# W' from high and low halves in three float32r passes instead of one float32 pass, its depth sum split in two

## The chip, the cores and the metric

The program runs on one core of a Trainium2 chip. The metric is device time in microseconds (us): the median of three runs. The profile is of one further execution; its span is the time from its first instruction to its last.

## The reference, cut to what matters

A clustered attention is followed by two feed-forward blocks. The change is in the last: `moe2_w3` and `moe2_w_out` are multiplied with nothing between them, so that the kernel may form their product first.

```python
def _moe2_ref(x, w1, w2, w3, w_out):      # x: 1536 x 512
    a = x @ w1                            # 512 x 1024
    b = x @ w2                            # 512 x 1024
    h = a * b @ w3                        # 1024 x 1024
    return (h @ w_out).astype(np.float32) # 1024 x 512
```

Ahead of it stand, for each of 2 batches, 8 heads of 768 rows and 64 columns: scores of q and k, masked to equal clusters, an exponential, a product with v; and a first feed-forward block `g(x @ w_in) @ w_out` with `g(h) = h` above 1, `(h + 1)^2 / 4` between, 0 below -1. The weights of both blocks come as 64-bit floats.

## The kernel before, in words

**Stages.** Attention of batch 0 is computed first (4 units of two heads, 48 score tiles of 128 x 768). Then the matmuls of both feed-forward blocks for batch 0 (line L1254) run between the score tiles of batch 1, and then those for batch 1 (L1254 and, in a form with fewer products, L1507). L1254 of batch 0 needs the whole of batch 0's attention.

**A score tile** is: four matmuls into PSUM (L853, TensorE, "PE"), a row maximum (L861, VectorE, "DVE"), a bias (L866, GpSimd, "POOL"), the exponential (L874, ScalarE, "ACT"), six transposes (L891, PE), a copy of the result to `pt` (ACT or DVE). Six tiles make a group, after which L962 multiplies with v (24 matmuls into `av`).

**Weights.** A chunk of 128 x 512 weights is loaded as 64-bit words (`w64`) and turned into float32 in `wf` by five instructions: absolute value of the high word (ACT, L1107), clamp (L1111), rebase (L1117) and sign (L1123) on DVE, low word by DVE (L1129) or by ACT and POOL (L1136, L1140). Where a chunk is used in float32r (a float32 that TensorE reads at less than full precision), it is split: the high half is a copy to float32r (`hi`, L347 on ACT or L349 on DVE), the low half is the chunk less its high half (`lo`, L352 on POOL or DVE), both in a `whl` tile. Three matmuls, high-high, high-low and low-high (`PASSES`), then stand for one float32 product (`mm4`, L1254).

**W'.** The product `w3 @ w_out` (1024 x 512) is made during batch 0's attention, in 8 blocks `m` of 128 rows, each in two steps `hf` of four depth tiles (`wp_mm`, L1198). The steps are in full float32: the chunk of w3 in `wf`, `w_out` in the tile `wo2` (8 depth tiles, 128 x 512 float32). The two steps of a block add up in one PSUM bank (`mo`), a copy takes it to `wf` (`wp_copy`), a DMA to the DRAM tensor `wp` (`wp_put`, L1211); the output matmuls read it back much later. PE's time for one step is that of 4 matmuls (the trace has 2 records for each, so x8).

**What sets the order.** Every operation is entered in a plan with its needs; the order in which all are issued, and for operations with two possible engines the engine, stand in a table written out in the program (`ORDER`). Each engine runs its part in that order and waits at each instruction for what it needs. DMAs are issued from ACT's queue (weights) and SP's (the rest).

## Time and profile before

| | |
|---|---|
| median of 3 runs | 726.48 us (725.79 to 728.29) |
| profiled execution | 725.32 us |
| its span | 723.6 us |
| PE, weight loads, DVE busy | 704.4, 617.9, 615.9 us |
| ACT, POOL busy | 465.5, 285.3 us |

Busy time is the union of an engine's instructions. Two records of one engine can overlap: the next starts before the last result is out. PEld is PE's loading of weights, which runs beside its matmuls. The chain of waits goes back from the last instruction to whatever let each step start; of it 89% is PE.

### The profile page before, as it was taken

Reading aid. Unit: us, or ns where it says so; the run is one execution under the profiler, and the core shown is the slowest. Engines: PE = TensorE matmul, PEld = TensorE weight load, DVE = VectorE, ACT = ScalarE, POOL = GpSimd, SP = SyncE. Lnnn points to the kernel's source line nnn. Section 1 sums busy time; section 2 is a strip of 40 time slices with the busy share of each in tenths; the row PEclk is TensorE's granted clock in tenths of the full one; section 3 lists DMA queues with packets and bytes.
Section 4 is the critical chain, followed back from the end, with each engine's and each line's share of the span. In section 5 each row is a group of like instructions: output and inputs, shape, how many; then the busy total and the mean of one; then the engine's idle time right before and its main releaser. Section 6 shows DMA issues by size and latency. Waiting matters only on the chain.

```text
span 723.6 us, 11965 instructions
## 1 busy us (share of the span) xinstructions
PE 704.4 (97%) x4144; PEld 617.9 (85%) x4145; DVE 615.9 (85%) x1134; ACT 465.5 (64%) x870; POOL 285.3 (39%) x358
## 2 busy tenths in 40 slices
...
GB/s 312 135 193 131 194 192 272 202 191 201 205 166 199 171 175 217 233 235 187 244 217 225 205 230 157 186 164 152 46 103 57 59 88 59 44 72 74 73 52 80
DMA packets 113932, 115.80 MB, mean 160 GB/s; under 512 B 74128, under 2 KB 82768, under 8 KB 113872
## 3 DMA queue, kind: packets, MB, share of 16 engines
...
q8 instruction: 32, 0.52, 0.3%
...
## 4 chain that ended last, share of the span: by engine, by line
PE 89%; DVE 4%; ACT 3%; DMA 2%; issue 1%; SPq 0%; POOL 0%; ACTq 0%; POOLq 0%; DVEq 0%
PE mo L1254 36%; PE sc L1507 9%; PE sc L853 9%; PE mo L1198 7%; PE mo L1507 5%; PE sc L891 5%; PE sc L1254 5%; PE av L962 4%; PE av L970 3%; PE av L1507 2%; PE av L1254 2%; DMA vn<-phl 1%; DMA kq<-in_qT_dram 1%; DVE nm L861 1%; ACT pt L347 1%
## 5 line engine op out<-in xcount | busy, mean ns | idle before, releaser
L1254 PE MATMUL mo<-X,whl 128*128 128x384 f32 x924 | 169.5, 338 | 0.0
L1254 PEld LDWEIGHTS mo<-X,whl 128*128 128x128 f32 x924 | 159.5, 188 | 2.3 <-issue 0.6
L1254 PE MATMUL mo<-G,whl 128*128 128x384 f32 x732 | 133.2, 337 | 0.0
L1254 PEld LDWEIGHTS mo<-G,whl 128*128 128x128 f32 x732 | 126.6, 188 | 0.9 <-DVE X L352 0.3
L861 DVE TENSOR_REDUCE nm<-sc 128x1 f32<-128x768 f32 x96 | 90.2, 952 | 15.9 <-PE sc L853 13.6
L352 POOL TENSOR_TENSOR whl<-wf,whl 128x512 fp32r<-128x512 f32 x48 | 63.3, 1319 | 73.1 <-ACT whl L347 44.6
L1140 POOL TENSOR_TENSOR wf<-wf,w 128x512 int32<-128x512 int32 x32 | 42.2, 1320 | 80.4 <-DVE wf L1123 32.1
L866 POOL TENSOR_SCALAR nm<-nm 128x1 f32<-128x1 f32 x96 | 26.3, 274 | 102.9 <-DVE nm L861 94.2
L347 ACT ACTIVATE whl<-wf 128x512 fp32r<-128x512 f32 x76 | 47.5, 627 | 29.4 <-PE mo L1254 11.8
L853 PE MATMUL sc<-k,q 128*128 128x512 f32 (+1 forms) x192 | 55.1, 368 | 3.8 <-DVE nm L861 1.6
L1198 PE MATMUL mo<-wo,wf 128*128 128x512 f32 x128 | 58.0, 596 | 0.0
L874 ACT ACTIVATE P<-sc,nm 128x768 f32<-128x768 f32 x56 | 50.1, 898 | 10.6 <-POOL nm L866 5.5
L347 ACT ACTIVATE pt<-sc 128x768 f32<-128x768 f32 (+1 forms) x50 | 39.4, 807 | 18.6 <-PE sc L891 14.7
L853 PE MATMUL sc<-kq 80*128 80x512 f32 (+1 forms) x192 | 49.7, 340 | 0.0
L891 PEld LDWEIGHTS sc<-ident,P 128*128 128x128 f32 x336 | 37.9, 141 | 12.5 <-issue 4.9
L1107 ACT ACTIVATE wf<-w 128x512 f32<-128x512 f32 x64 | 42.4, 672 | 5.7 <-POOL wf L1140 1.7
L891 PE MATMUL sc<-ident,P 128*128 128x128 f32 x336 | 43.9, 275 | 1.6 <-DVE nm L861 1.3
L1123 DVE SCALAR_TENSOR_TENSOR wf<-w,wf 128x512 uint32<-128x512 uint32 x64 | 44.2, 693 | 0.9
L874 ACT ACTIVATE sc<-sc,nm 128x768 f32<-128x768 f32 x40 | 34.7, 868 | 15.5 <-POOL nm L866 15.4
L1198 PEld LDWEIGHTS mo<-wo,wf 128*128 128x128 f32 x128 | 23.3, 190 | 24.5 <-issue 23.7
L352 DVE TENSOR_TENSOR phl<-sc,phl 128x768 f16<-128x768 f32 x40 | 38.1, 952 | 5.6 <-ACT phl L347 5.2
L853 PEld LDWEIGHTS sc<-k,q 128*128 128x128 f32 x192 | 31.4, 189 | 12.2 <-DVE nm L861 3.0
...
## 6 DMA issues: line engine op xcount, KB each, us to landing
wf<-wd ACTq DMA_DIRECT2D x64, 256.0 KB, 2.7
...
wd<-wf SPq DMA_DIRECT2D x48, 256.0 KB, 3.6
...
wf<-wp ACTq DMA_DIRECT2D x16, 256.0 KB, 2.9
...
```

The source lines that it names most:

```text
L347: nc.scalar.activation(out=out, in_=in_, func=AF.Copy)
L352: (nc.gpsimd if e == "POOL" else nc.vector).tensor_tensor(out=out, in0=a, in1=b, op=ALU.subtract)
L853: nc.tensor.matmul(ps[:, n], q[0:n_rows, q0:q0 + 128], k[0:n_rows, n], start=first, stop=not first)
L861: nc.vector.tensor_reduce(out=nm, in_=T[("sc", b), s], axis=AX.X, op=ALU.max, negate=True)
L874: nc.scalar.activation(out=new(("P", b), s).rearrange("p n s -> p (n s)") if by_pe(s) else T[("sc", b), s], in_=T[("sc", b), s], func=AF.E ...
L891: nc.tensor.transpose(T[("sc", b), s][:, c], p[:, c], ident)
L1107: nc.scalar.activation(out=T["wf", i], in_=T[w64, i].bitcast(F32)[:, :, 1], func=AF.Abs)
L1123: nc.vector.scalar_tensor_tensor(out=w, in0=T[w64, i][:, :, 1], scalar=0xC0000000, in1=w, op0=ALU.bitwise_and, op1=ALU.bitwise_or)
L1140: nc.gpsimd.tensor_tensor(out=w, in0=w, in1=T[w64, i].bitcast(I32)[:, :, 0], op=ALU.add)
L1198: nc.tensor.matmul(acc, w[:, k4 * 128:(k4 + 1) * 128], wo2[:, hf * 4 + k4], start=(hf == 0 and k4 == 0), stop=(hf == 1 and k4 == 3),)
L1254: nc.tensor.matmul(acc, w[:, a, k4 * 128:(k4 + 1) * 128], rhs(c, k4), start=(first and k4 == 0 and n == 0), stop=(last and k4 == 3 and n = ...
L1507: nc.tensor.matmul(ps, lhs(av, a, k), rhs(bv, c, k), start=k == 0 and n == 0, stop=k == 1 and n == 2,)
```

## The change

The steps of W' run in three float32r passes. The chunks of w3 (16) and of w_out2 (8) are split into halves: 24 more copies and 24 more subtractions. Split w_out2 takes twice the room, so that the depth sum is made in two parts: first `hf` 0 of all 8 blocks, then `hf` 1. The first part is copied from PSUM to `wf` and stored in a DRAM tensor `wp0`; it is loaded back, added to the second part on DVE, and stored in `wp`. Only four split depth tiles are kept at a time: two in parts of `X0` that attention fills later (its last two units now wait for the first part), the others in tiles of their own. `ORDER` is another table.

In the order, `sc` tiles are scores, `mo` the PSUM bank of W', `X_75` and `wo_119` to `wo_122` the homes of split w_out2; lines of the changed kernel are 6 higher for the operations of attention. On PE, a place behind the third product with v, before:

```order
L891 MATMUL sc_178<-ident,P_108 128x128 x6
L1198 MATMUL mo_123<-wo_118,wf 128x512 x4
L891 MATMUL sc_177<-ident,P_106 128x128 x6
L891 MATMUL sc_177<-ident,P_107 128x128 x6
L1198 MATMUL mo_123<-wo_118,wf 128x512 x4
L783 MATMUL sc_178<-ident,raw_91 128x128 x6
L853 MATMUL sc_177<-k_98,q_101 128x512
```

and in the changed kernel:

```order
L897 MATMUL sc_181<-ident,P_107 128x128 x6
L897 MATMUL sc_182<-ident,P_109 128x128 x6
L1194 MATMUL mo_127<-X_75,whl 128x512 x6
L1194 MATMUL mo_127<-wo_119,whl 128x512 x3
L1194 MATMUL mo_127<-wo_120,whl 128x512 x3
L897 MATMUL sc_181<-ident,P_108 128x128 x6
L859 MATMUL sc_182<-k_99,q_102 128x256
```

A step is 4 float32 matmuls before and 12 float32r matmuls now, with as many transposes around it.

On DVE, in the fifth group of score tiles (between the 25th and the 26th row maximum, L861 and L867), before:

```order
L861 TENSOR_REDUCE nm<-sc_178 128x1
L1111 TENSOR_SCALAR wf<-wf 128x512
L1117 TENSOR_SCALAR wf<-wf 128x512
L1123 SCALAR_TENSOR_TENSOR wf<-w_115,wf 128x512
L1129 SCALAR_TENSOR_TENSOR wf<-w_115,wf 128x512
L1111 TENSOR_SCALAR wf<-wf 128x512
L352 TENSOR_TENSOR X_75<-av,X_75 128x384
L1111 TENSOR_SCALAR wf<-wf 128x512
L1117 TENSOR_SCALAR wf<-wf 128x512
L1123 SCALAR_TENSOR_TENSOR wf<-w_111,wf 128x512
L861 TENSOR_REDUCE nm<-sc_177 128x1
```

and now:

```order
L867 TENSOR_REDUCE nm<-sc_182 128x1
L355 COPY rb<-mo_127 128x384
L1132 SCALAR_TENSOR_TENSOR wf<-w_112,wf 128x512
L987 TENSOR_TENSOR av<-av,rb 128x384
L358 TENSOR_TENSOR k_100<-kq_118,k_100 64x768
L358 TENSOR_TENSOR whl<-wf,whl 128x512
L358 TENSOR_TENSOR wo_122<-wf,wo_122 128x512
L358 TENSOR_TENSOR q_103<-kq_118,kq_106 64x768
L936 TENSOR_SCALAR su<-su 128x6
L937 RECIPROCAL rc<-su 128x6
L1114 TENSOR_SCALAR wf<-wf 128x512
```

Low halves (L358 to `whl` and `wo`) stand between the conversions, the row maxima and the work on k and q.

On ACT, in the same group, before:

```order
L347 ACTIVATE wf<-mo_123 128x512
L874 ACTIVATE P_106,su<-sc_177,nm 128x768
L347 ACTIVATE vn<-sc_178 128x768
L347 ACTIVATE rb<-mo_123 128x384
L347 ACTIVATE pt_96<-sc_177 128x768
L1136 ACTIVATE w_115<-w_115 128x512
L874 ACTIVATE P_107,su<-sc_177,nm 128x768
L874 ACTIVATE P_108,su<-sc_178,nm 128x768
```

and now:

```order
L353 ACTIVATE whl<-wf 128x512
L353 ACTIVATE pt_97<-sc_182 128x768
L880 ACTIVATE P_107,su<-sc_182,nm 128x768
L353 ACTIVATE kq_106<-kq_118 64x768
L353 ACTIVATE wf<-mo_127 128x512
L1139 ACTIVATE w_112<-w_112 128x512
L353 ACTIVATE rb<-mo_127 128x384
L1104 DMA w_115<-in_w_out_dram 128x1024
L353 ACTIVATE whl<-wf 128x512
```

High halves (L353 `whl<-wf`) and further copies of k and q stand between the exponentials (L880) and the copies to `pt`.

Between the 6th and the 30th tile the order has on DVE 8 more low halves, 1 more high half, 3 more copies from PSUM to `wf` and 8 more conversion instructions; on ACT 12 more high halves, 6 more copies of k and q and 3 more absolute values. Between the 30th and the 48th tile it has on DVE the 8 additions, and 2 copies to `wf`, 3 copies to `pt` and 2 low parts of k and q fewer; on ACT 7 more high halves and 3 more copies to `pt`. On PE the 16 steps stand 8 and 8 in both stretches, before and now. Of the 24 low halves 11 are on DVE and 13 on POOL; of the 24 high halves 21 on ACT and 3 on DVE.

```diff
--- before.py
+++ after.py
@@ -36,63 +36,65 @@
...
 ORDER = (
-    "##$V$.$0$4#%#*$X$2#,#0$]#.$Z%s%X%V%Z#(%e#2#4%h%k$6%c$_%y&,%r:m%_$H$8%m$::|$a;.$<%a;<$q%|$c$>%i#_$J&%#i#e$e%u"
...
+    "###%#<#*$X$V$.$0#,#0$4$2#.%X:m%V%e#(#2%[#4%c%q%h$6$8%_;%$:%y%m%b$_%|&#$H$<$Z$]$q%i%]$a$c#:#c$>:o;6$@$e$B$F&,"
...
@@ -192,6 +194,7 @@
     tri = const.tile([128, 128], BF16, name="tri")
     half = const.tile([128, 1], F32, name="half")
     nbig = const.tile([128, 1], F32, name="nbig")
+    wp0 = dram.tile([KF2, 128, DM], F32, name="wp0")
     wp = dram.tile([DM // 128, 128, KF2, 128], F32, name="wp")
     xd = dram.tile([KD, 128, S], F32, name="xd")
 
@@ -217,7 +220,10 @@
             RINGS[r, b] = len(BUFS[r, b])
     mask0 = early_p.tile([128, 2, 2, TG], F32R, name="mask0")
     kq0 = early_p.tile([128, 2, NP, S], F32, name="kq0")
-    wo2 = early_p.tile([128, KF2, DM], F32, name="wo2")
+    BUFS["wo2"] = [early_p.tile([128, 2, DM], F32R, name=f"wo2{i}") for i in range(KF2 // 2)]
+    RINGS["wo2"] = KF2 // 2
+    BUFS["wo2x"] = [X0[:, :, j, :DM] for j in (KD - 1, KD - 2)]
+    RINGS["wo2x"] = 2
     late = {}
 
 
@@ -284,7 +290,7 @@
     ROWS, ROW, MASK = ((0.45, 1.24),), ((0.45, 0.57),), ((0.75, 0.45),)
     MOVES = {
         "c_load": ((0.45, 0.18),), "al": ROWS, "ul": ROWS, "vl": ROWS, "ap": ROWS, "vT": ((0.62, 2.7),),
-        "sT": ((0.62, 2.7),), "k2": ROW * 2 + MASK, "wps": ((0.45, 1.05),), "wd": ((0.45, 1.05),),
+        "sT": ((0.62, 2.7),), "k2": ROW * 2 + MASK, "wps": ((0.45, 1.05),), "wps0": ((0.45, 1.05),), "wpl": ((0.45, 1.05),), "wd": ((0.45, 1.05),),
         "xs": ROW, "xr": ROW, "os": ROW,
     }
 
@@ -1070,7 +1076,7 @@
             nm = ("x", u, g)
             add(("xm", u, g), {"DVE": 0.5}, p + 3.0, x_mul(u, g), [("pv", u, g), ("ri", u, g)], [("tmp", nm)] if b else [], [("av", (u, g)), ("rb", (u, g))] if b else [("rb", (u, g))], near=("av", (u, g)))
             if b == 0:
-                add_split("x", nm, p + 3.5, lambda a, j=j, g=g: X0[:, a, j, cols(g)], [("xm", u, g)], "av", (u, g))
+                add_split("x", nm, p + 3.5, lambda a, j=j, g=g: X0[:, a, j, cols(g)], [("xm", u, g)] + ([("wp", m, 0) for m in range(KF2)] if j >= KD - 2 else []), "av", (u, g))
             else:
                 add(("xs", u, g), {"DMA": 0.5}, p + 4.0, to_dram(nm, xd[j, :, cols(g)]), [("xm", u, g)], frees=[("tmp", nm)])
 
@@ -1082,13 +1088,13 @@
 
 
     nchunk = [0]
-    N_EARLY = 2 * KF2 + wo2.shape[1] + AHEAD
+    N_EARLY = 3 * KF2 + AHEAD
     c64 = []
 
     def low_by_pool(i):
         return i % 2 == 0
 
-    def chunk(t, src, is64, split=True, dst=None, needs=(), keep=None):
+    def chunk(t, src, is64, split=True, halves="whl", needs=(), keep=None):
         i = nchunk[0]
         nchunk[0] += 1
         w64 = ("w64", 0 if i < N_EARLY else 1)
@@ -1100,10 +1106,7 @@
                 nc.scalar.dma_start(out=new("wf", i), in_=src)
 
         def absv(e):
-            if dst is None:
-                new("wf", i)
-            else:
-                T["wf", i] = dst
+            new("wf", i)
             nc.scalar.activation(out=T["wf", i], in_=T[w64, i].bitcast(F32)[:, :, 1], func=AF.Abs)
 
         def clamp(e):
@@ -1143,10 +1146,10 @@
             nc.sync.dma_start(out=wd[keep], in_=T["wf", i])
 
         def hi(e):
-            copy(e, new("whl", i)[:, 0], T["wf", i])
+            copy(e, new(halves, i)[:, 0], T["wf", i])
 
         def lo(e):
-            w = T["whl", i]
+            w = T[halves, i]
             sub(e, w[:, 1], T["wf", i], f(w)[:, 0])
 
         if is64:
@@ -1158,7 +1161,7 @@
             if before is not None:
                 needs = list(needs) + [(LAG_W, ("wc", before, 3))]
             add(("wl", i), {"ACT": 0.2}, t - 14.0, load, list(needs) + W_AFTER[i:i + 1], [(w64, i)], behind="w64", moves=((0.46, 1.8),))
-            add(("wabs", i), {"ACT": 0.56}, t - 9.0, absv, [("wl", i)], [] if dst is not None else [("wf", i)], behind="wf")
+            add(("wabs", i), {"ACT": 0.56}, t - 9.0, absv, [("wl", i)], [("wf", i)], behind="wf")
             add(("wc", i, 0), {"DVE": 0.34, "POOL": (1.92, LATE)}, t - 8.6, clamp, [("wabs", i)])
             add(("wc", i, 1), {"DVE": 0.34}, t - 8.2, rebase, [("wc", i, 0)])
             add(("wc", i, 2), {"DVE": 0.6}, t - 7.8, top, [("wc", i, 1)])
@@ -1174,36 +1177,45 @@
             add(("wl", i), {"ACT": 0.2}, t - 12.0, load, needs, [("wf", i)], behind="wf", moves=((0.46, 1.05),))
             last = ("wl", i)
         if split:
-            add(("whi", i), {"ACT": 0.52, "DVE": (0.34, LATE)}, t - 5.0, hi, [last], [("whl", i)], behind="whl")
+            add(("whi", i), {"ACT": 0.52, "DVE": (0.34, LATE)}, t - 5.0, hi, [last], [(halves, i)], behind=halves)
             add(("wlo", i), {"POOL": 1.3, "DVE": (0.61, LATE)}, t - 4.0, lo, [("whi", i)], frees=[("wf", i)])
         return i
 
 
 
-    W_ACC = [("mo", 0), "av", ("sc", 0), ("sc", 0)][:W_SIDE] + [("mo", 0)] * (KF2 - W_SIDE)
-
-    def wp_acc(m, first=False):
-        ring, name = W_ACC[m], ("wp", m)
-        t = new(ring, name) if first else T[ring, name]
-        if ring == ("sc", 0):
-            o = 0 if where[ring, name] % PER[0] == 0 else S - 512
-            t = t[:, o:o + 512]
-        return t
-
-    def wp_mm(i, m, hf):
-        def fn(e):
-            w = T["wf", i]
-            acc = wp_acc(m, hf == 0)
+    def wo2_home(kt):
+        return "wo2x" if kt < 2 else "wo2"
+
+    def wp_mm(i, m, hf, x):
+        def fn(e):
+            w, acc = T["whl", i], new(("mo", 0), ("wp", m, hf))
             for k4 in range(4):
-                nc.tensor.matmul(
-                    acc, w[:, k4 * 128:(k4 + 1) * 128], wo2[:, hf * 4 + k4],
-                    start=(hf == 0 and k4 == 0), stop=(hf == 1 and k4 == 3),
-                )
-        return fn
-
-    def wp_copy(m):
-        def fn(e):
-            copy(e, new("wf", ("wp", m)), wp_acc(m))
+                for n, (a, c) in enumerate(PASSES):
+                    nc.tensor.matmul(
+                        acc, w[:, a, k4 * 128:(k4 + 1) * 128], T[wo2_home(hf * 4 + k4), x[k4]][:, c],
+                        start=(k4 == 0 and n == 0), stop=(k4 == 3 and n == 2),
+                    )
+        return fn
+
+    def wp_part(m):
+        def fn(e):
+            copy(e, new("wf", ("wp0", m)), T[("mo", 0), ("wp", m, 0)])
+        return fn
+
+    def wp_keep(m):
+        def fn(e):
+            nc.sync.dma_start(out=wp0[m], in_=T["wf", ("wp0", m)])
+        return fn
+
+    def wp_back(m):
+        def fn(e):
+            nc.sync.dma_start(out=new("wf", ("wp", m)), in_=wp0[m])
+        return fn
+
+    def wp_add(m):
+        def fn(e):
+            w = T["wf", ("wp", m)]
+            nc.vector.tensor_tensor(out=w, in0=w, in1=T[("mo", 0), ("wp", m, 1)], op=ALU.add)
         return fn
 
     def wp_put(m):
@@ -1215,30 +1227,28 @@
 
     dt = DT_W
     wo2_chunks = []
-    steps = [(m, hf) for hf in range(2) for m in range(W_SIDE)] + [(m, hf) for m in range(W_SIDE, KF2) for hf in range(2)]
+    WO2_AT = {0: range(4), 3: (4,), 5: (5,), 8: (6, 7)}
+    steps = [(m, hf) for hf in range(2) for m in range(KF2)]
     for n, (m, hf) in enumerate(steps):
         t = T_W + dt * n
-        if m == 0:
-            for kt in range(hf * 4, hf * 4 + 4):
-                wo2_chunks.append(chunk(t - 10.0 + 2.0 * (kt % 4), w_out2[kt], True, False, wo2[:, kt]))
-        i = chunk(t, w3T[m, hf], True, False)
-        needs = [("wc", i, 3)] + [("wc", x, 3) for x in wo2_chunks[hf * 4:hf * 4 + 4]]
-        if hf:
-            needs.append(("wp", m, 0))
-        elif W_ACC[m] == ("sc", 0):
-            needs.append(("am", 0, "q", NP - 1))
+        for kt in WO2_AT.get(n, ()):
+            wo2_chunks.append(chunk(t - 10.0 + 2.0 * (kt % 4), w_out2[kt], True, True, wo2_home(kt)))
+        x = wo2_chunks[hf * 4:hf * 4 + 4]
+        i = chunk(t, w3T[m, hf], True, True)
+        acc = (("mo", 0), ("wp", m, hf))
         add(
-            ("wp", m, hf), {"PE": 3.44}, t, wp_mm(i, m, hf), needs,
-            [(W_ACC[m], ("wp", m))] if hf == 0 else [], [("wf", i)],
+            ("wp", m, hf), {"PE": 2.8}, t, wp_mm(i, m, hf, x), [("wlo", i)] + [("wlo", y) for y in x],
+            [acc], [("whl", i)] + [(wo2_home(hf * 4 + k4), y) for k4, y in enumerate(x)],
         )
         while ahead and len(ahead) * 2 * KF2 > AHEAD * (2 * KF2 - 1 - n):
             x, src = ahead.pop(0)
             chunk(t + dt / 2, src, True, False, keep=x)
-        if hf:
-            add(
-                ("wpe", m), {"ACT": 0.5, "DVE": (0.61, LATE)}, t + dt, wp_copy(m), [("wp", m, 1)],
-                [("wf", ("wp", m))], [(W_ACC[m], ("wp", m))],
-            )
+        if hf == 0:
+            add(("wpe0", m), {"ACT": 0.5, "DVE": (0.61, LATE)}, t + dt, wp_part(m), [("wp", m, 0)], [("wf", ("wp0", m))], [acc])
+            add(("wps0", m), {"DMA": 0.5}, t + dt + 2.0, wp_keep(m), [("wpe0", m)], frees=[("wf", ("wp0", m))])
+        else:
+            add(("wpl", m), {"DMA": 0.5}, t - 4.0, wp_back(m), [("wps0", m)], [("wf", ("wp", m))])
+            add(("wpe", m), {"DVE": 0.61}, t + dt, wp_add(m), [("wp", m, 1), ("wpl", m)], frees=[acc])
             add(("wps", m), {"DMA": 0.5}, t + dt + 2.0, wp_put(m), [("wpe", m)], frees=[("wf", ("wp", m))])
 
 
```

## Rows read from the trace of the kernel before

**Rows 1.** Five stretches of the program: busy time by engine (clock, DMA share, GB/s last)
```profile
core 0: us, PE busy (x) PEld busy (x) DVE busy (x) ACT busy (x) POOL busy (x), PEclk, DMA share, GB/s
0.00:44.00 44.00, 30.94 (x207) 21.99 (x209) 35.01 (x76) 36.01 (x55) 16.46 (x28) 1.00 0.61 209
44.00:127.00 83.00, 82.75 (x427) 52.38 (x424) 73.58 (x121) 70.23 (x121) 27.86 (x41) 1.00 0.61 202
127.00:200.00 73.00, 72.01 (x387) 42.50 (x388) 65.81 (x111) 53.61 (x94) 18.16 (x30) 1.00 0.64 199
200.00:475.00 275.00, 273.53 (x1729) 257.25 (x1728) 244.27 (x416) 198.94 (x367) 117.85 (x141) 1.00 0.86 200
475.00:723.60 248.60, 245.16 (x1403) 243.78 (x1402) 197.21 (x413) 106.71 (x236) 104.96 (x120) 1.00 0.26 82
```

**Rows 2.** Chain of waits, 93 to 202 us: start us, length us, what
```profile
93.11 3.66 PE mo L1198 x8
96.77 1.31 PE sc L891 x12
98.08 3.44 PE mo L1198 x8
...
115.75 0.69 PE sc L853 x4
...
122.94 0.81 ACT pt L347
123.78 0.85 ACT kq L347
...
187.92 3.44 PE mo L1198 x8
...
200.07 2.11 PE mo L1254 x12
```

**Rows 3.** Groups by line: operation, tiles, shapes, count | busy us, mean ns | idle before
```profile
L1254 PE MATMUL mo<-X,whl 128*128 128x384 f32 x924 | 169.5, 338 | 0.0
L1254 PEld LDWEIGHTS mo<-X,whl 128*128 128x128 f32 x924 | 159.5, 188 | 2.3 <-issue 0.6 <-DVE tmp L1279 0.3 <-ACT tmp L347 0.3
L352 POOL TENSOR_TENSOR whl<-wf,whl 128x512 fp32r<-128x512 f32 x48 | 63.3, 1319 | 73.1 <-ACT whl L347 44.6 <-DVE whl L349 18.8 <-issue 5.6
L347 ACT ACTIVATE whl<-wf 128x512 fp32r<-128x512 f32 x76 | 47.5, 627 | 29.4 <-PE mo L1254 11.8 <-PE sc L1254 4.8 <-PE mo L1507 4.0
L352 DVE TENSOR_TENSOR whl<-wf,whl 128x512 fp32r<-128x512 f32 x48 | 34.5, 721 | 1.9 <-ACT whl L347 1.8
L1107 ACT ACTIVATE wf<-w 128x512 f32<-128x512 f32 x64 | 42.4, 672 | 5.7 <-POOL wf L1140 1.7 <-issue 1.0 <-DVE whl L352 0.8
L1123 DVE SCALAR_TENSOR_TENSOR wf<-w,wf 128x512 uint32<-128x512 uint32 x64 | 44.2, 693 | 0.9
L1111 DVE TENSOR_SCALAR wf<-wf 128x512 f32<-128x512 f32 x61 | 26.1, 429 | 2.8 <-ACT wf L1107 2.0 <-POOL G L352 0.4 <-issue 0.2
L1289 DVE TENSOR_TENSOR Yp<-Yp,mo 128x384 f32<-128x384 f32 x29 | 15.4, 545 | 0.0
L347 ACT ACTIVATE kq<-kq 64x768 fp32r<-64x768 f32 x17 | 14.2, 840 | 0.6 <-PE sc L853 0.3
```

**Rows 4.** Waits of VectorE, then of ScalarE, 44 to 127 us: total us, times, longest
```profile
DVE nm L861 <- PE sc L853: 5.3, 6, 1.2
ACT pt L347 <- PE sc L891: 3.1, 6, 0.7
```

**Rows 5.** Timeline at 86 us, VectorE and GpSimd: start us, length us, what
```profile
85.50 0.69 DVE L1123 SCALAR_TENSOR_TENSOR wf<-w,wf 128x512 uint32<-128x512 uint32 x1
...
86.32 1.29 POOL L1140 TENSOR_TENSOR wf<-wf,w 128x512 int32<-128x512 int32 x1 [4.76 <-DVE wf L1123]
...
86.97 1.20 DVE L1123 SCALAR_TENSOR_TENSOR wf<-w,wf 128x512 uint32<-128x512 uint32 x1
```

**Rows 6.** DMA issues of W' to and from DRAM: count, size, median us to landing
```profile
wf<-wp ACTq DMA_DIRECT2D x16, 256.0 KB, 2.9
...
wp<-wf SPq DMA_DIRECT2D x8, 256.0 KB, 4.6
```

More of the change, by code (lines that the diff above doesn't have):

```diff
@@ L94 @@
[L94 to L95 removed]
+    "###%#<#*$X$V$.$0#,#0$4$2#.%X:m%V%e#(#2%[#4%c%q%h$6$8%_;%$:%y%m%b$_%|&#$H$<$Z$]$q%i%]$a$c#:#c$>:o;6$@$e$B$F&,"
+    "$J$s$L#m#w$*#D#L#e#@$g$i;H;X:q$N:w$D:s#_$k#s#B#q$,%s$(:u:y%u#F#i#|$%$u$o$P$m#g#N#8$R;(;*)u&($w$##6#V#Z%o#a#y"
+    ";,;8%k%w$T)w)y;m:|;c&*$y$|)|;.;0;2;4;:;<*4*(*##R#u#><%#k***,#o*%*6*8;@;>;B*.;J*@*B%#*0*:*L;L;N;E;P;$*D*F*<#]"
```

112 lines of the change are left out of this document (56 added, 56 removed).

## The prediction

> **What bounds the kernel now.** I read the page first, then busy time by stretch, the chain of waits, the groups by line, the waits of two engines, one piece of the timeline and the DMA issues.
>
> The stretches [rows 1] are cut at 44 us (the sixth score tile's exponential), at 127 us (the thirtieth), at 200 us (the first matmul of L1254) and at 475 us (the end of attention). The reader is to see that PE is busy nearly throughout from 44 us on, that DVE is at 89% and 90% of the two stretches in which W' is made, and that ACT is at 85% of the first of them and 73% of the second.
>
> PE's busy time alone proves little, since its records overlap. The chain is better evidence [rows 2]: the step of W' that starts at 93.11 us ends where twelve transposes start, and these end where the next step starts (93.11 + 3.66 = 96.77, 96.77 + 1.31 = 98.08). Between 44 and 121 us the chain is almost all of this kind, so PE's own work is what sets the pace there, and a step of 3.44 us is 3.44 us of path. The exception is 122 to 132 us, where the chain runs through one ACT instruction after another (two of them are shown). The last step ends at 191.4 us, and at 200.07 us L1254 starts. From there on PE is the bound: 273.5 of 275 us busy, then 245.2 of 248.6.
>
> **The change, part by part.** The sum is made against the profiled execution, 725.3 us (723.6 of span and 1.7 around it); the median is 1.2 us above it.
>
> PE, the 16 steps. A step takes 3.44 us now. The trace has no float32r pass of 512 columns for W'; the nearest rows [rows 2] are 12 passes of 384 columns in 2.11 us, 0.234 us per 512 columns, and the four passes of a score tile, 1,536 columns in 0.69 us, 0.230. Twelve passes are then 2.81 or 2.76 us, a step is 0.63 to 0.68 us shorter, 16 steps 10.1 to 10.9 us. I take 10.1, 5.0 in each stretch since 8 steps stand in each. Could the weight loads (12 a step, not 4) undo this? In the group of L1254 924 loads of 188 ns lie beside 924 matmuls that take 169.5 us together [rows 3]; a matmul of 0.234 us covers a load of 0.188.
>
> The price is on the other engines, all of it before 200 us. By the groups [rows 3]: a high half is 0.63 us on ACT, a low half 0.72 on DVE or 1.32 on POOL, an addition from PSUM 0.545 x 512 / 384 = 0.73 on DVE (an estimate from the row of 384 columns).
>
> First stretch, 44 to 127 us (tiles 6 to 30 in the order). DVE: 8 low halves 5.8, one high half 0.5, 3 copies out of PSUM at 0.73 make 2.2, 8 more conversion instructions between 0.43 and 0.69 make 4.0; the copies of transposed scores and of v that come from ACT and the casts of k and q that go there about cancel (+0.5). Sum 13. ACT: 12 high halves 7.5, 6 more copies of k and q at 0.84 make 5.0, 3 more absolute values at 0.67 make 2.0, less 1.8 for what goes to DVE. Sum 12.7. So DVE has 73.6 + 13 = 86.6 us and ACT 70.2 + 12.7 = 82.9 us of work for a stretch that lasts 83 us, while PE falls by 5.0. The cover that DVE had is gone: it was idle 9.4 us, of which 5.3 were waits for score matmuls [rows 4], which a relieved PE shortens, as it does ACT's waits for transposes (3.1). With the other 4.1 kept the stretch is 90.7 us (+7.7). The other end: consecutive instructions that don't need each other start before the last one's end, so that 13 us of added durations may add only 11, and with no idle time left the stretch is 84.6 (+1.6). I take +5.
>
> Second stretch, 127 to 200 us. DVE: 8 additions 5.8, less 2 copies of W' 1.5, 3 copies to `pt` 2.7, 2 low parts of k and q 2, and some smaller ones 2: about -2.4. ACT +3.3, but it has 19 us idle there. PE -5.0. The stretch becomes 2.4 to 5 us shorter. Each step now hands the one PSUM bank on through a copy or an addition, and the next step and the small transposes into the same bank (L948) are queued on PE behind it; in most places one or two sets of transposes (0.66 us each by the 1.31 us of two [rows 2]) lie between two steps, which about covers 0.7 us. Where only one does, PE may wait some tenths, 1 us in all. I take 3.
>
> The last two units' attention output now waits for the first part of W' to leave its home in `X0`. ACT's and DVE's further work is queued behind that wait. In PE's order all 8 steps of the first part stand ahead of the fifth product with v, whose result is the first to wait, so nothing is added; if they were late, the price is a step, 2.8 us.
>
> DMA: 8 stores and 8 loads of 256 KB more; such transfers land in 4.6 and 2.9 us [rows 6], and the DMA engines are 61 to 64% busy there [rows 1]. The loads back stand in SP's queue several places ahead of their additions, with stores of converted weights queued behind them. What hides them is the distance between the two parts of a block, 8 steps. Nothing is added; if a late landing were to hold a `wf` tile, the price is one landing, 3 to 5 us.
>
> POOL gets 13 low halves, 17 us, where it has 46 us of work in 156. It waits far more than it works, so I cost it at nothing for itself. But [rows 5] show an effect on DVE: an instruction of L1123 that takes 0.69 us takes 1.20 when it starts inside a POOL instruction on SBUF tiles: POOL's ends at 86.32 + 1.29 = 87.61 us, DVE's at 88.17, as if it had done most of its work only then.
>
> The Trainium skill's page "SBUF — State Buffer", section "Who interferes with whom", says why: VectorE with two SBUF inputs, or in its two-port modes, shares a port pair with GpSimd, and the later one waits for all of the other. The rows just read agree. The rule speaks against this change, which adds instructions on both sides of that port; by it the time would be that of the second rival below.
>
> After 200 us the same matmuls run in the same number, PE stays the bound, and what the new order shifts between DVE and POOL lies beside PE: 0, with 3 us either way for another packing.
>
> Sum: +5 - 3 = +2 before 200 us and 0 after: 727.3 for the profiled execution, 728.5 for the median. Ends of this case: +1.6 - 5.0 = -3.4 and +7.7 - 2.4 = +5.3.
>
> **Rivals.**
> PE's gain comes through. For it: the chain is PE nearly everywhere, and busy time overstates DVE and ACT, since consecutive instructions overlap; DVE could take its 86.6 us in less than 83 if few of them stood alone. Against it: 86.6 us of DVE work in 83, and DVE was busy for no more than 89 or 90% in any of the stretches [rows 1]. Between 3.4 and 10.1 us come out; the time is 726.5 - 6 = 720.5.
>
> DVE is held by POOL (slower). Each of the 13 low halves on POOL meets a DVE instruction on SBUF tiles behind it. The place is the two W' stretches, the price 1.20 - 0.69 = 0.51 us each, 6.6 us; some of them meet row maxima from PSUM, so that 5.5 remain: 728.5 + 5.5 = 734. It decides once more than half of them delay a row maximum on the path. For it: DVE has no slack to take it up in the first stretch. Against: the mean of L1123 over the whole trace, 0.693 us [rows 3], is its undelayed length, so that such delays are rare now.
>
> The steps don't get shorter: a pass would have to pay its load, 0.234 + 0.188, 5.1 us a step and 26 us in all. The loads of L1254 lie beside the matmuls, so this gets one in a hundred.
>
> **How the numbers follow.** The even exchange (-3.4 to +5.3 us around +2) 0.42, the gain comes through 0.30, POOL holds DVE 0.27, longer steps 0.01. What a measurement of this kernel can tell is about 0.3%, 2.2 us. Of the even exchange 0.05 is faster than that, 0.20 within, 0.17 slower. Faster: 0.30 + 0.05 = 0.35, shaded to 0.34; same 0.21; slower 0.17 + 0.27 + 0.01 = 0.45. The likeliest case's own range is 723 to 732; the range that is to hold the time 8 times in 10 reaches to 718 (most of the gain) and 736.
>
> **What would show it.** Steps: the group of `wp_mm` with 12 matmuls in about 2.8 us, and PE with more idle time before 200 us than now. Exchange: the first L1254 between 197 and 205 us, DVE above 93% and ACT above 90% between the sixth and thirtieth tile, and the chain there with more ACT and DVE pieces. Gain: L1254 starts at 196 us or before. POOL: low halves on POOL with lengthened DVE instructions behind them, DVE's mean for L1123 and L352 above 0.69 and 0.72. I am wrong in another way if the stretches after 200 us differ by over 3 us, or if SP or a `wf` tile holds a conversion.

## The result, and the profile after

The changed kernel takes 730.35 us (median of 7 runs, 729.73 to 733.01) against 726.48 us of the kernel before: a ratio of 1.0065, with a 95% interval of 1.0045 to 1.0084. It is slower by about 4.7 us by the ratio. The profiled execution took 733.01 us (span 731.3), the longest of the seven and 2.7 us above their median, and the execution profiled before was 1.2 us under its own. So the 7.7 us between the two spans overstate the loss by about 3 us, and so do the stretches below.

The changed file's numbers differ: the steps of W' are L1194 (before L1198), the later matmuls L1264 (L1254), absolute values L1110 (L1107), L1126 answers to L1123, low halves L358 (L352), copies L353 and L355 (L347, L349), row maxima L867, exponentials L880, transposes L897, scores L859. New are the store of a first part, L1207, its load back, L1212, and its addition, L1218.

Busy time of the changed kernel in the stretches of [rows 1], cut at the same events (sixth and thirtieth exponential, first L1264, end of attention; columns as there; tiles and exponentials are counted from 0):

```profile
0.00:43.30 43.30, 33.09 (x209) 22.75 (x211) 35.88 (x75) 35.55 (x54) 15.35 (x27) 1.00 0.56 200
43.30:131.60 88.30, 80.02 (x452) 60.07 (x449) 78.68 (x137) 80.70 (x139) 36.80 (x47) 0.96 0.63 209
131.60:208.60 77.00, 72.52 (x421) 50.58 (x420) 67.60 (x113) 56.13 (x98) 34.81 (x39) 0.96 0.70 218
208.60:474.50 265.90, 265.85 (x1666) 249.62 (x1664) 248.00 (x420) 189.34 (x353) 124.09 (x143) 1.00 0.86 206
474.50:731.30 256.80, 253.02 (x1469) 250.98 (x1468) 202.09 (x413) 104.13 (x233) 117.99 (x133) 1.00 0.27 83
```

The first matmul of the later block starts at 208.6 us instead of 199.8, and behind it the span is 522.7 us instead of 523.8: all of the loss lies before it. The first stretch of W' is 88.3 us long (before 83, by its rounded cuts), the second 77.0 (before 73); by the times of the trace nine of the sixteen steps start in the first and seven in the second, now as before. DVE has 78.7 us of work in the first of them, 5 more than before, and ACT 80.7, 10.5 more. The third column from the end is new: the granted clock is 0.96 in both.

Two of the groups of [rows 3] in the changed kernel. POOL makes more of the low halves, and the mean durations of these two are as in [rows 3] (1330 for 1319 ns, 693 for 693):

```profile
L358 POOL TENSOR_TENSOR whl<-wf,whl 128x512 fp32r<-128x512 f32 x63 | 83.7, 1330 | 94.6 <-ACT whl L353 42.7 <-DVE whl L355 36.7 <-issue 11.0
...
L1126 DVE SCALAR_TENSOR_TENSOR wf<-w,wf 128x512 uint32<-128x512 uint32 x72 | 49.4, 693 | 0.6
```

The loss is not spread evenly. These are the two stretches of W' cut at the exponentials of tiles 26 and 35, before and now:

```profile
44.00:112.40 68.40, 68.15 (x364) 43.26 (x361) 61.09 (x103) 57.70 (x100) 20.45 (x33) 1.00 0.56 186
112.40:145.80 33.40, 32.92 (x170) 18.59 (x169) 29.95 (x46) 27.30 (x46) 12.63 (x15) 1.00 0.70 228
145.80:199.80 54.00, 53.48 (x279) 32.83 (x279) 48.14 (x84) 38.64 (x68) 12.95 (x23) 1.00 0.66 202
```

```profile
43.30:109.20 65.90, 63.84 (x381) 46.80 (x378) 61.78 (x110) 62.18 (x108) 26.50 (x36) 1.00 0.61 198
109.20:155.30 46.10, 38.03 (x196) 27.48 (x195) 37.41 (x61) 33.12 (x57) 21.92 (x21) 0.85 0.68 228
155.30:208.60 53.30, 50.68 (x299) 36.37 (x298) 47.09 (x81) 41.53 (x74) 23.20 (x30) 1.00 0.71 218
```

Up to tile 26 the changed kernel is 2.5 us faster, with DVE and ACT both busy for 94% of the time, and behind tile 35 it is 0.7 us faster. From tile 26 to tile 35 it takes 46.1 us for 33.4, 12.7 us more, with DVE at 81%, ACT at 72%, and a granted clock of 0.85.

Slices of 10 us show that piece more closely: first two of the kernel before, then five of the changed kernel.

```profile
110.00:120.00 10.00, 10.00 (x40) 5.69 (x40) 8.28 (x11) 8.34 (x16) 6.03 (x7) 1.00 0.74 238
120.00:130.00 10.00, 10.00 (x51) 6.08 (x51) 8.64 (x16) 8.86 (x14) 4.92 (x6) 1.00 0.74 258
```

```profile
110.00:120.00 10.00, 7.27 (x43) 6.08 (x41) 8.43 (x17) 7.91 (x16) 4.21 (x6) 1.00 0.81 275
120.00:130.00 10.00, 6.51 (x23) 5.30 (x24) 6.10 (x10) 8.51 (x15) 4.91 (x4) 0.71 0.68 229
130.00:140.00 10.00, 10.00 (x47) 6.28 (x47) 7.52 (x14) 6.43 (x12) 2.31 (x4) 0.78 0.33 102
140.00:150.00 10.00, 8.74 (x67) 5.42 (x66) 9.90 (x15) 6.08 (x11) 6.13 (x4) 1.00 0.89 299
150.00:160.00 10.00, 8.72 (x42) 6.96 (x42) 9.06 (x16) 7.05 (x14) 5.29 (x7) 0.83 0.66 224
```

Before, PE did not stand still here. Now it stands still for 6.2 us between 110 and 130, and then the granted clock falls to the lower of its two levels (1.2 GHz) for 13.7 us in all between 120.8 and 155.0. No engine is full where PE stands still: from 120 to 130 us DVE is at 61% and ACT at 85%. So here a chain of waits costs the time, not a sum of work. PE's two longest waits there, from its timeline (the bracket holds the idle time and its releaser):

```profile
121.12 1.54 PE L897 MATMUL sc<-ident,P 128*128 128x128 f32 x6 [3.84 <-ACT P L880]
...
126.95 0.61 PE L859 MATMUL sc<-k,q 128*128 128x256 f32 x2 [2.12 <-ACT k L353]
```

And the chain of waits of the same kernel, from 111 us (start us, length us, what):

```profile
111.17 0.70 DVE wf L355
111.88 5.00 DMA wp<-wf
...
116.97 0.68 ACT wf L1110
...
117.67 0.80 DVE wf L1114
118.47 0.88 DVE nm L867
...
130.11 4.86 PE mo L1194 x12
...
141.74 0.33 SPq L1212
142.16 5.98 DMA wd<-wf
...
148.22 0.67 ACT wf L1110
...
178.62 2.77 PE mo L1194 x12
```

A step takes 2.77 us in the last of these lines, 3.44 in [rows 2]; one at the low clock took 4.86. Behind 111 us stands something that the chain before did not have: a first part is copied into a `wf` tile (L355), its store lands 5.0 us later, and only then may ACT's absolute value (L1110) take that tile. ACT works in order, so tile 29's exponential, which PE's transposes wait for, stands behind it; and on DVE that tile's row maximum (L867) stands behind the clamp (L1114) that waits for the same absolute value. Of the eight stores of first parts, which land in 2.0 to 5.4 us, this is the only one that an engine is seen waiting for. At 141.7 us a load back (L1212) that had waited for a tile of its own is issued, the store of a converted weight queued behind it in SP lands at 148.1, and L1110 waits again. ACT's longest waits between 90 and 160 us:

```profile
ACT wf L1110 <- DMA wd<-wf: 2.9, 1, 2.9
...
ACT wf L1110 <- DMA wp<-wf: 1.9, 2, 1.6
```

### The profile page after: what moved, and what is told of

The parts are those of the page before. It is cut to its first block, busy times and chain, and to the rows that moved or that the text cites. A ratio compares the mean times of both kernels' runs of the same rounds, so it can differ in the third digit from the quotient of the medians.

```text
span 731.3 us, 12227 instructions
## 1 busy us (share of the span) xinstructions
PE 704.5 (96%) x4208; PEld 634.0 (87%) x4209; DVE 632.2 (86%) x1153; ACT 465.8 (64%) x876; POOL 329.1 (45%) x389
## 4 chain that ended last, share of the span: by engine, by line
PE 83%; DVE 6%; DMA 4%; ACT 3%; issue 2%; POOL 1%; ACTq 0%; SPq 0%; DVEq 0%; POOLq 0%
PE mo L1264 38%; PE sc L859 8%; PE sc L1517 8%; PE sc L1264 6%; PE mo L1517 5%; PE mo L1194 4%; PE av L968 4%; PE av L976 3%; PE sc L897 3%; DMA kq<-in_qT_dram 2%; PE av L1517 2%; PE av L1264 2%; DVE nm L867 1%; ACT pt L353 1%; DMA wd<-wf 1%
## 5 line engine op out<-in xcount | busy, mean ns | idle before, releaser
L1264 PE MATMUL mo<-X,whl 128*128 128x384 f32 x912 | 167.2, 337 | 0.0
L1264 PEld LDWEIGHTS mo<-X,whl 128*128 128x128 f32 x912 | 157.2, 188 | 2.7 <-issue 0.9
L1264 PE MATMUL mo<-G,whl 128*128 128x384 f32 x696 | 127.1, 337 | 0.1
L358 POOL TENSOR_TENSOR whl<-wf,whl 128x512 fp32r<-128x512 f32 x63 | 83.7, 1330 | 94.6 <-ACT whl L353 42.7
L1264 PEld LDWEIGHTS mo<-G,whl 128*128 128x128 f32 x696 | 120.1, 188 | 1.4 <-DVE Yp L1299 0.4
L867 DVE TENSOR_REDUCE nm<-sc 128x1 f32<-128x768 f32 x96 | 90.0, 950 | 14.6 <-PE sc L859 8.2
L1143 POOL TENSOR_TENSOR wf<-wf,w 128x512 int32<-128x512 int32 x36 | 52.2, 1449 | 92.4 <-DVE wf L1126 29.6
L353 ACT ACTIVATE whl<-wf 128x512 fp32r<-128x512 f32 x87 | 54.4, 628 | 34.5 <-PE mo L1264 13.3
L859 PE MATMUL sc<-k,q 128*128 128x512 f32 (+1 forms) x192 | 55.2, 369 | 5.0 <-ACT k L353 2.1
L880 ACT ACTIVATE P<-sc,nm 128x768 f32<-128x768 f32 x56 | 50.2, 900 | 10.3 <-POOL nm L872 7.7
L1110 ACT ACTIVATE wf<-w 128x512 f32<-128x512 f32 x72 | 47.2, 672 | 13.5 <-DMA wd<-wf 2.9
L859 PE MATMUL sc<-kq 80*128 80x512 f32 (+1 forms) x192 | 51.0, 348 | 0.3 <-ACT kq L353 0.3
L897 PE MATMUL sc<-ident,P 128*128 128x128 f32 x336 | 44.6, 278 | 5.6 <-ACT P L880 4.4
L897 PEld LDWEIGHTS sc<-ident,P 128*128 128x128 f32 x336 | 38.0, 142 | 13.7 <-ACT P L880 7.7
L1126 DVE SCALAR_TENSOR_TENSOR wf<-w,wf 128x512 uint32<-128x512 uint32 x72 | 49.4, 693 | 0.6
L353 ACT ACTIVATE pt<-sc 128x768 f32<-128x768 f32 (+1 forms) x49 | 38.7, 812 | 10.8 <-PE sc L897 8.8
L880 ACT ACTIVATE sc<-sc,nm 128x768 f32<-128x768 f32 x40 | 34.7, 866 | 16.3 <-POOL nm L872 16.2
L859 PEld LDWEIGHTS sc<-k,q 128*128 128x128 f32 x192 | 32.1, 194 | 14.6 <-ACT pt L353 4.2
L1194 PE MATMUL mo<-wo,whl 128*128 128x512 f32 x144 | 39.1, 420 | 0.8 <-DVE wf L1218 0.8
L358 DVE TENSOR_TENSOR phl<-sc,phl 128x768 f16<-128x768 f32 x40 | 37.9, 949 | 1.8 <-ACT phl L353 1.6
L358 DVE TENSOR_TENSOR whl<-wf,whl 128x512 fp32r<-128x512 f32 x49 | 34.8, 714 | 4.3 <-ACT whl L353 3.8
```

The lines of the kernel that those rows point to most:

```text
L353: nc.scalar.activation(out=out, in_=in_, func=AF.Copy)
L358: (nc.gpsimd if e == "POOL" else nc.vector).tensor_tensor(out=out, in0=a, in1=b, op=ALU.subtract)
L859: nc.tensor.matmul(ps[:, n], q[0:n_rows, q0:q0 + 128], k[0:n_rows, n], start=first, stop=not first)
L867: nc.vector.tensor_reduce(out=nm, in_=T[("sc", b), s], axis=AX.X, op=ALU.max, negate=True)
L880: nc.scalar.activation(out=new(("P", b), s).rearrange("p n s -> p (n s)") if by_pe(s) else T[("sc", b), s], in_=T[("sc", b), s], func=AF.E ...
L897: nc.tensor.transpose(T[("sc", b), s][:, c], p[:, c], ident)
```

## The experiments

Five theories of the loss. 1: a `wf` tile is held through a landing, and ACT's queue waits for it. 2: the sum of DVE's and ACT's work, as predicted. 3: the clock that falls after PE has stood still. 4: POOL holds DVE at a port. 5: the places in the queues that the new order gave. Ratios are to the kernel before in the same runs, with 95% intervals; the changed kernel stands at 1.0065 (1.0045 to 1.0084).

| kernel | median us | ratio |
|---|---|---|
| e_1pass | 730.18 | 1.0083 (1.0050 to 1.0117) |
| e_nolo | 731.78 | 1.0065 (1.0044 to 1.0086) |
| e_nostore | 727.92 | 1.0014 (0.9999 to 1.0029) |
| e_stage | 729.65 | 1.0040 (1.0023 to 1.0057) |
| e_stage8 | 729.30 | 1.0035 (1.0019 to 1.0052) |
| e_idle | 735.14 | 1.0121 (1.0098 to 1.0144) |
| e_idle2 | 729.72 | 1.0044 (1.0025 to 1.0064) |
| e_order | 731.70 | 1.0060 (1.0045 to 1.0075) |
| e_tuned | 729.00 | 1.0019 (1.0004 to 1.0034) |
| e_tuned2 | 727.87 | 1.0024 (1.0003 to 1.0046) |
| e_tuned_idle | 727.50 | 1.0008 (0.9984 to 1.0032) |
| b_short (from the kernel before) | 723.32 | 0.9959 (0.9937 to 0.9981) |

**Is it PE, or the work on the halves?** Two kernels take work away.

```diff
-                for n, (a, c) in enumerate(PASSES):            # e_1pass, in wp_mm
+                for n, (a, c) in enumerate(PASSES[:1]):
...
```

> The changed kernel with one pass (high half by high half) instead of three in each of the 16 steps of W', everything else kept (two thirds of W's products are left out): a step falls from 2.78 to about 0.93 us, 29.6 us of PE's work less. If PE set the end of the stretch before 200 us: 701 to 715 us. Theory 1 and 2 (ACT, DVE and the landings set it): 727 to 731 us, PE stands still longer; theory 3: the clock may fall for longer, which costs nothing where PE has room.

```diff
         def lo(e):                                             # e_nolo, in chunk
+            if is64 and keep is None:
+                return
...
```

> The changed kernel without the 24 low halves of W2_out's and W3's chunks (11 on DVE at 0.68 us, 13 on POOL at 1.3 us); all 12 matmuls of a step remain and read the high halves in their place (two of three products of W' are wrong values, none is left out). Theory 2: 7.4 us of DVE's and 17 us of POOL's work go, the sum of the first stretch falls by about 5.4 us of DVE's: 725 to 727 us. Theory 4 (POOL's low halves hold DVE at the shared port): the same direction, and DVE's instructions beside them get shorter. Theory 1 (landings hold `wf` tiles): a tile of a chunk comes free a little earlier, the waits for landings stay: 728.5 to 730.5 us.

Neither moved the time. Of e_1pass these are the stretch from the sixth to the thirtieth exponential and the wait that costs PE most between 43 and 204 us (16.0 us in 11 times); of e_nolo the same stretch:

```profile
43.20:132.00 88.80, 69.64 (x388) 49.11 (x384) 78.35 (x137) 80.63 (x140) 37.08 (x48) 0.91 0.65 208
...
PE sc L897 <- ACT P L880: 16.0, 11, 4.3
```

```profile
43.40:130.40 87.00, 79.31 (x451) 59.01 (x448) 74.23 (x128) 80.44 (x139) 29.87 (x42) 0.96 0.64 212
```

With 10.4 us less on PE the stretch of e_1pass is as long as it was (88.8 for 88.3 us), and PE waits for exponentials instead. In e_nolo DVE has 4.5 us less and POOL 6.9 than the changed kernel, the stretch is 1.3 us shorter, and later waits take that back. So DVE's part of theory 2 falls, and theory 4 with it: the low halves cost nothing that can be measured. ACT's part was taken away by no run. Up to tile 26, where ACT is busy for 94% of the time, e_1pass (66.8 us) and e_nolo (65.9) are no faster than the changed kernel (65.9), so there ACT's work may set the pace. It is not what makes the loss: that piece is faster than before, and in the piece that loses 12.7 us ACT is at 72%.

**What the `wf` tiles cost.** Three kernels change the home of a first part: no stores and loads at all, another home ahead of the store, another home on both sides.

```diff
-            nc.sync.dma_start(out=wp0[m], in_=T["wf", ("wp0", m)])          # e_nostore
...
-            nc.sync.dma_start(out=new("wf", ("wp", m)), in_=wp0[m])
+            new("wf", ("wp", m))
...
```

> The changed kernel without the 8 stores of the first part to `wp0` and without the 8 loads back; each first part is still copied out of PSUM into a `wf` tile at its place, each `wf` tile of a load back is still taken at its place, and the addition still runs on DVE with a constant in place of the first part (so the first part's sum is left out of W'). Theory 1 (a `wf` tile that waits for a landing of the store or the load stops ACT's queue at 112 and 142 us, then PE): the two waits of 5 to 6 us go, first mm4 matmul at about 201 instead of 208.6 us, 721 to 725 us. Theory 2 (the sum of DVE's and ACT's work in 44 to 127 us, as predicted): the same work remains on both, 729 to 731.5 us. Theory 3 (TensorE's granted clock falls after a stall, and the 13.7 us at the low level cost 6.8 us): the clock stays high only if the stall goes, so as theory 1, or 730 if the stall has another cause.

```diff
-            copy(e, new("wf", ("wp0", m)), T[("mo", 0), ("wp", m, 0)])      # e_stage
+            copy(e, kq0[:, m % 2, 0, :DM], T[("mo", 0), ("wp", m, 0)])
...
-            nc.sync.dma_start(out=new("wf", ("wp", m)), in_=wp0[m])         # and in e_stage8
+            nc.sync.dma_start(out=part(m, True), in_=wp0[m])                # kq0[:, m % 2, m // 2, :DM] for m > 0
...
```

> All work of the changed kernel; only the home of the first part between PSUM and DRAM moves: instead of a `wf` tile it is the raw K or Q of batch 0's first unit (free after its halves are made), two places in turn, and the loads of batch 1's K and Q into these two places stand behind the last of the 8 stores in SP's queue. The loads back still take `wf` tiles. Theory 1: no absolute value waits for the store's landing any more, the stall at 117 us goes (4 to 5 us) and that at 142 us, which hangs on a load back, stays: 724 to 727 us. Theory 2: 729 to 731.5 us. Theory 3: 724 to 727 us if the clock stays high after the stall that is gone, and no low clock in 120 to 135 us.

> All work of the changed kernel, and no `wf` tile held for the first part any more, but for the first load back: the first parts leave PSUM into the raw K and Q of batch 0's first unit, as in e_stage, and the loads back of the 2nd to 8th first part go into seven other places of the raw K and Q of batch 0 (free after batch 1's block means are made), where they are added and stored from. The second load back stands behind those means' matmuls. Theory 1 (what a `wf` tile is held for): as little waiting as without the stores and loads at all (e_nostore, 727.92 us), so 726 to 728.5 us; if loads back that stand ahead of a `wd` store in SP's queue cost of themselves, not the tile, it stays near e_stage's 729.65. Theory 2 (the sum of DVE's and ACT's work): nothing of it changes, 729 to 731.5 us.

e_nostore is faster than the changed kernel, with intervals apart: 1.0065 - 1.0014 = 0.0051, 3.7 us (some 2 to 5.5 us by the two intervals). So the transfers, which I had costed at nothing, cost about 3.7 us, three quarters of the loss. Its 727.92 us lie above what theory 1 expected (721 to 725). The two staged kernels lie between, their intervals overlap the changed kernel's, and both came out above what theory 1 expected: part of the cost seems to be the transfers' own and not the tile's, which these runs don't separate. The wait itself is gone, though. In e_nostore ACT's absolute value that took the stored tile starts at 115.33 us instead of 116.97 and waits for nothing; PE's stall behind it falls only from 3.84 to 2.48 us, in e_nostore as in e_stage8. First the absolute value in e_nostore, then PE's wait in e_stage8:

```profile
115.33 0.68 ACT L1110 ACTIVATE wf<-w 128x512 f32<-128x512 f32 x1
```

```profile
119.68 0.88 PE L897 MATMUL sc<-ident,P 128*128 128x128 f32 x6 [2.48 <-ACT P L880]
```

**The places in the queues.** What is left of that stall is order: tile 29's row maximum stands behind conversion steps on DVE, its exponential behind two copies on ACT. And the changed order puts the scores of tile 31 behind the last unit's K and Q conversions, which write the ring place that the tile reads, so that PE waits for them. In that one tile it then multiplies the later unit's high halves: a fault of the order, not only a wait. Seven operations were moved (the expectation says eight, one too many), tile 31's scores among them; the code of none changes.

```diff
+        done = plan.order()
+        for x, y in [(("smax", 29), ("s", 29)), (("sbias", 29), ("smax", 29)), (("sexp", 29), ("wr", 24)),
+                     (("s", 31), ("s", 32)), (("sT", 28), ("wc", 24, 1)),
+                     (("wpe", 0), ("wc", 26, 2)), (("wps", 0), ("wpe", 0))]:
+            op = done.pop([n for _, _, n, _ in done].index(x))
+            done.insert([n for _, _, n, _ in done].index(y) + 1, op)
...
```

> All work of the changed kernel, with eight operations moved in the order of work, on engines that stand still or run others' work ahead of them in its trace at 111 to 135 us: tile 29's row maximum, bias and exponential go ahead of other chunks' conversions (the transposes of PE waited for that exponential); tile 31's scores stand ahead of the last unit's K and Q conversions, which take over the ring place that the tile still reads (PE waited 2.1 us for them); tile 28's copy goes ahead of two conversions on DVE; the first addition of W' and its store go behind nine conversion steps on DVE (DVE waited 2.45 us for that step's matmuls with them behind it). Theory 5 (the searched order holds the queues: what stands behind a waiting instruction loses the time, and no engine's sum does): the stalls of 3.8 and 2.1 us on PE shrink, 725 to 728 us. Theory 1 (landings of stores that hold `wf` tiles): the stall at 117 us is the landing's and stays, 729 to 731 us. Theory 3 (the clock): falls with the stalls, as theory 5.

> The moves of e_order on top of e_stage8 (no `wf` tile held for first parts but one), with the second load back right behind the K means' matmuls, one place further up in SP's queue. Theory 5 with theory 1 (both cost, on their own): e_stage8's 729.3 less 3 to 5 us: 724 to 727 us, at or under the kernel before. Theory 1 alone: 728.5 to 730 us. If the stalls only move on to the next wait in the same stretch: 728 to 730 us, with the first of the later block's matmuls at 204 us or later (before 199.8).

> e_tuned with tile 29's row maximum seven conversion steps further up in DVE's order and its exponential right behind tile 28's on ACT (in e_tuned's trace the maximum still ran at 117.0 us, behind seven conversion steps, though the scores were there at 114.1), and tile 28's copy two steps later (it held DVE for 1.34 us). Theory 5 (the place in the queues sets it): PE's wait of 3.2 us for tile 29 goes, no low clock behind it, 2 to 5 us less than e_tuned (ratio 1.0019): 724 to 727 us against 727 of the kernel before. Rival (the stall moves on: the tiles behind wait for the conversions that are now later): 728 to 730 us.

By themselves the moves changed nothing (1.0060). On top of e_stage8 they gave 1.0019, apart from the changed kernel but not from e_stage8. Moving further, in e_tuned2, changed nothing again: PE's wait for tile 29 fell from 3.2 to 1.8 us, and one of 2.2 us came 20 us later, where e_tuned had 0.7. PE's two longest waits of e_tuned2 between 90 and 205 us:

```profile
PE sc L531 <- ACT pt L353: 2.2, 1, 2.2
PE sc L897 <- ACT pt L353: 2.0, 2, 1.8
```

So the moves are shown to gain only together with the staging, and how much of that gain is theirs is not shown. The waits of e_tuned2 bear out its rival, that the stall moves on; its 727.87 us lie just under the rival's range (728 to 730) and above theory 5's (724 to 727).

**The clock.** Idle matmuls hold TensorE busy through the stalls.

```diff
+            for _ in range({("spT", 29): 15, ("s", 31): 9, ("ah", 1, "k", 4, None): 4, ("ro", 2, 0): 2}.get(name, 0)):
+                idle_mm("PE")                                  # e_idle2; e_idle: 34, 20, 10, 5
...
```

> The changed kernel with 69 idle matmuls of 128x128 (about 0.11 us each, nothing reads them) put ahead of the PE instructions that stood still in its trace: 34 ahead of the transposes that waited from 117 to 121 us, 20 ahead of the scores that waited from 124.5 to 127, 15 in two places at 148 to 151 us. They hold TensorE busy through the stalls. Theory 3: the granted clock stays at 1.0 from 120 to 155 us, and the time falls by up to 6.8 us: 723.5 to 728 us. Theory 1 and theory 2 (the stalls are ACT's, PE has room to catch up): 729 to 732 us, with or without the low clock.

> As e_idle with 30 idle matmuls in place of 69, since each took 0.228 us there, not 0.11, and they ran on past the stalls (7.76 us ahead of a wait of 3.8): 15, 9, 4 and 2 in the same four places, each shorter than the stall that the changed kernel's trace shows. Theory 3: the granted clock is at 1.0 from 120 to 155 us and the time falls to 724 to 728 us. Theories 1 and 2 (PE has room in these stretches, what it gains ends in another wait): 729 to 731.5 us though the clock stays at 1.0.

> e_tuned with 13 idle matmuls (3.0 us at 0.228 us) ahead of the transposes of tile 29, where PE stood still for 3.2 us at 118 us and the granted clock was low for the 10.2 us behind it (122.6 to 132.8). Theory 3 (the clock by itself): clock at 1.0 throughout, PE's work of these 10.2 us takes half the time, up to 5 us less than e_tuned: 724 to 727 us. Theory 5 (the queues of ACT and DVE set the pace there, PE has room): 728 to 730 us.

e_idle was a miss of mine: each matmul took 0.228 us, twice what I had read from a record, and they held PE for 7.8 us where it would have waited 3.8. e_idle2 kept the clock up until 149.7 us in its profile and cannot be told from the changed kernel (1.0044). In its profiled execution e_tuned_idle kept it up; over all twelve the mean granted clock was 1.00 in five (median 727.0 us) and 0.995 to 0.998 in the others. The slices from 120 and 130 us, of e_tuned and of e_tuned_idle:

```profile
120.00:130.00 10.00, 7.68 (x27) 6.16 (x28) 9.25 (x12) 8.45 (x13) 6.28 (x7) 0.63 0.89 281
130.00:140.00 10.00, 9.37 (x51) 5.74 (x49) 6.88 (x14) 7.46 (x14) 2.05 (x3) 0.86 0.61 192
```

```profile
120.00:130.00 10.00, 7.42 (x44) 6.16 (x43) 9.26 (x12) 8.89 (x14) 6.30 (x7) 1.00 0.91 286
130.00:140.00 10.00, 7.61 (x56) 4.01 (x59) 7.60 (x17) 7.82 (x14) 1.95 (x3) 1.00 0.66 213
```

10.2 us at the low level is 5.1 us of PE's work. With it gone the first later matmul starts 1.2 us earlier in these two profiles (203.3 for 204.5 us), and PE is idle for 2.4 us in a slice where it had been busy for 9.37: about three quarters of the price were hidden under the same waits. The ratios, 1.0019 and 1.0008, don't tell the two apart. By the profiles theory 3 is worth about 1 us here; the intervals would also admit nothing, or some 3 us.

**What the shorter steps are worth alone.** The kernel before, with narrower matmuls:

```diff
+                n = 512 if hf == 0 and k4 == 0 else 384 if hf == 0 else 416
                 nc.tensor.matmul(
-                    acc, w[:, k4 * 128:(k4 + 1) * 128], wo2[:, hf * 4 + k4],
+                    acc[:, :n], w[:, k4 * 128:(k4 + 1) * 128], wo2[:, hf * 4 + k4, :n],
...
```

> The kernel before, with 1664 columns instead of 2048 in each of the 16 half steps of W' (the first matmul of a part whole, the others on 384 or 416 of 512 columns; these products are left out of W'): a half step takes about 2.80 us instead of 3.44, as the changed kernel's does, and nothing is added or moved: no low halves, no store and load of a first part, the same order. It prices the PE term alone, 16 times 0.64 us = 10.2 us. If PE's 100% between 90 and 180 us is the whole bound there: first matmul of the later block at 189.6 instead of 199.8 us, 715 to 719 us. If the other engines' waits stand right behind PE's in that order too: 720 to 724.5 us. If nothing comes through: 725 to 727 us.

A step took 2.80 us, as wanted, and of the 10.2 us that PE saves 3.0 came through (0.0041 of 726.2 us; 1.4 to 4.6 by the interval); in the profile the first later matmul starts at 196.7 instead of 199.8 us. The chain says why. Its shares by line from 85 to 200 us, before and in b_short:

```profile
by line: PE mo L1198 33.6%; PE av L962 17.5%; PE sc L891 17.0%; PE sc L853 16.1%; ACT pt L347 2.9%; ACT wf L1107 1.8%; ACT P L874 1.6%; PE mo L948 1.6%; ACT kq L347 1.5%; PE sc L525 1.3%; PE sc L783 1.1%; DVE nm L861 0.8%; ACT q L347 0.7%; 
```

```profile
by line: PE av L962 10.5%; PE sc L853 7.5%; PE sc L891 7.5%; issue 5.6%; ACT P L874 5.1%; DVE nm L861 4.8%; DMA w<-in_w3T_dram 3.2%; ACT kq L347 2.5%; PE mo L1199 2.4%; DVE wf L1123 2.2%; ACT wf L1107 2.2%; ACT pt L347 2.2%; PE mo L1255 2.1
```

The steps' share falls from 33.6 to 2.4%. The chain had been PE's, with exponentials, row maxima and loads of weights directly behind it.

## Why the prediction was right, and where it was not

It said 728.5 us with slower the likeliest sign; 730.35 lies in its range and in the even exchange's own. The mechanism was not the one forecast, and that the terms nearly made up the total is partly luck: in the profiles the first stretch, the second and the rest came out at +5, +4 and -1 us where the sum had +5, -3 and 0. The first L1264 started at 208.6 us, outside the 197 to 205 named as the exchange's sign. By its terms:

- **The steps**: 2.81 us said, 2.77 measured at the full clock, with the weight loads beside the matmuls. The size was right, its worth was not: the shorter second stretch rested on it, and b_short shows that 3.0 of the 10.2 come through in the old order. (The prediction puts eight steps into each stretch; by the trace nine and seven start in them.) The chain [rows 2] had shown PE on the path; it could not show how closely the next engine followed.
- **First stretch, +5 from DVE's and ACT's sum**: the profile has +5 (88.3 for 83), but not for that reason. ACT got 10.5 us more (12.7 said), DVE 5.1 (13 said; it stayed at 89%, where 93% was the sign), and taking 4.5 us off DVE gave 1.3. Where both engines were at 94%, up to tile 26, the kernel was faster than before. The number fell in place by waits that I had not put there.
- **Second stretch, -3**: this step failed. It became 4 us longer (77.0 for 73), by a step at the low clock and by the waits behind 141 us. Without the transfers, in e_nostore, the clock stays at 1.00 in it and it is about as long as before:

```profile
129.80:203.20 73.40, 70.10 (x420) 48.38 (x420) 67.00 (x113) 56.12 (x98) 34.64 (x39) 1.00 0.63 205
```

- **The transfers at 0**: this failed too, and is the larger cause. I had written that a late landing that holds a `wf` tile costs 3 to 5 us and that eight steps of distance hide it. The distance hides the load from its addition; it does not hide the tile, which is taken from the same ring of four as the conversions. Taking the transfers out gave 3.7 us; how much of it is the tile's is not shown, since keeping the first parts out of the ring (e_stage8) gave 2.2 us with intervals that overlap.
- **After 200 us, 0**: -1.1 us, within the 3 allowed.
- **Rivals**: POOL as a brake is excluded by e_nolo and by L1126, 0.693 us as L1123 in [rows 3], and 0.68 us in both stretches of W' (L1123: 0.72 and 0.69). The port rule of the Trainium skill's page "SBUF — State Buffer", section "Who interferes with whom", stands: single instructions are held as in [rows 5]. Here they were few, by these means, and the 13 low halves on POOL can go without a gain. The gain that comes through is excluded by the result. "If SP or a `wf` tile holds a conversion", named as the way to be wrong otherwise, is what the chain shows.

The account: shown are 3.7 us for the transfers, and 3.0 us that the shorter steps gain in the old order; what they gain in the new one is not shown (in e_1pass still shorter steps gained nothing). If the two could be added, 4 us more would be left for the new order's waits and the clock behind them, an estimate that no run shows by itself. Staging, moves and idle matmuls together brought 1.0065 down to 1.0008, that is 4.1 us, but how it divides between order, clock and what staging alone gives stays open, since neighbouring kernels' intervals overlap. None of the versions with all products is faster than the kernel before; only b_short is, which leaves products out.
